# A decode step of attention beside a gated MLP: column groups of the output product, the last head's products and the final copy in two halves

## The chip, the cores and the metric

The kernel runs on one core of one Trainium2 chip. Its engines are TensorE (PE, with its weight loads as PEld), VectorE (DVE), ScalarE (ACT), GpSimd (POOL) and SyncE (SP); SyncE and ScalarE also issue DMA transfers, each on its own queue, and 16 DMA engines carry them. The metric is the device time in microseconds (us) of one execution. Before the change it was 662.07 us, the median of three runs (661.95 to 662.16).

## The reference

For a batch of 4 with one new token each (D = 640), the kernel adds three things:

```python
x = A_x                                    # 4 x 1 x 640, bf16
xn = _layernorm(x, axis=-1)
return x + _A_ref(xn, k_cache, v_cache, wq, wo) + _B_ref(xn, w_in, w_sp, b_sp, w_out)

# A: 32 heads of 128, caches of 4096 rows per batch and head
q = (x @ wq).reshape(B, 1, 32, 128)
p = softmax(q @ k.T * 128 ** -0.5)
return (p @ v).reshape(B, 1, 32 * 128) @ wo

# B: F = 1728, Fh = 864
z = gelu(x @ w_in)                         # tanh approximation
z1, z2 = z[..., :Fh], layernorm(z[..., Fh:])
return (z1 * (w_sp * z2 + b_sp)) @ w_out
```

The key and value caches are 4 x 32 x 4096 x 128 in bf16, 134 MB each. Everything else is small beside them.

## The kernel before

**Units.** The work is cut into 16 units: a group of 8 heads (`hg`, four of them) and one batch (`b`). A unit's keys are 8 x 4096 rows of 128, laid out over 128 partitions as 256 rows each (8 MB); its values likewise. Keys go to a ring of seven places in SBUF (`k_ring`, a quarter of a unit, 2 MB, in each place), values to `v_all`.

**Loads.** All loads of caches and weights go through SyncE's queue in a fixed list, `loads`. A function `pump()` issues as many of them as have their places free; every step of the main loop calls it. A place is taken when its load is issued and freed in the program once the last work that reads it has been put down; the instruction then waits by semaphore for that work. Ahead of the list stands the load of the query weights (L118). Behind the first two quarters of keys come the MLP's weights `w_in` (L127) and `w_out` (L124), which lie where values and products lie later. The first load of values (L175) can be issued only when the MLP is done with them. The last two units' loads are cut finer, so that the values of the last unit and the last group's output weights (L228, L231) come in pieces. The last head's weights come in two loads of 320 columns. The semaphores that count the landings of these loads are eight in number and are used in turn.

**Units in time.** In the main loop, VectorE multiplies a quarter of keys with the query, spread to all partitions (`product`, L537), and folds the product once (`fold_half`, L543); TensorE sums the rest with products against an identity (L555); VectorE reduces to scores (L569). Once a unit's scores are there, VectorE finds the maximum, ScalarE takes the exponentials (L596), VectorE spreads them by head (L607), and TensorE multiplies them with the values (L631). The order on TensorE, VectorE, ScalarE and SyncE is the one in which the program writes the instructions; GpSimd's is left to the scheduler.

**Start.** ScalarE's queue loads x (L101), TensorE puts x into the output sum (L373), VectorE computes the statistics (L265) and normalizes, TensorE transposes (L289) and multiplies with the query weights when they land (L303).

**The MLP.** `gmlp()` (L397) is a generator whose parts are put between the first steps of the main loop: products with `w_in` (L404), the tanh form of the GELU on VectorE and ScalarE (L414 to L432), the sums for its layer norm by a product with ones (L435), the statistics (L445 to L460), and the products with `w_out` (L503).

**The output sum.** One PSUM tile `out_ps` holds the output. Its 640 columns are held in two groups of 320: group 0 in partitions 0 to 3, group 1 in partitions 32 to 35 (`out_sum`, L369). x itself, the MLP and the four groups of heads (`group_proj`, L696) are summed into it by products of 320 columns for each group. The last group of heads ends the kernel: `o_n_last` (L817), 16 products (L699), one copy by ScalarE to SBUF (L823) and two transfers to the output, one from ScalarE's queue (L824) and one from SyncE's (L825).

Of the kernel before, what the change touches and what calls it, by code (L numbers as in the profile page):

```python
# [9 lines left out]
FP32 = mybir.dt.float32  # L10
BF16 = mybir.dt.bfloat16
ACT = mybir.ActivationFunctionType
ALU = mybir.AluOpType
# [4 lines left out]
def kernel(  # L18
# [14 lines left out]
    nc = tc.nc  # L33
    P = nc.NUM_PARTITIONS
    Bsz, Sq, D = A_x.shape
# [3 lines left out]
    Fh = F // 2  # L39
# [9 lines left out]
    HT = 8  # L49
    PAR = HT // NQ  # L50
    LN = P // HT
    HG = H // HT
# [17 lines left out]
    NOH = D // 2  # L70
# [10 lines left out]
    const = ctx.enter_context(tc.tile_pool(name="const", bufs=1))  # L81
# [18 lines left out]
    x_bf = ring[0:Bsz, 1, 0:D]  # L100
    nc.scalar.dma_start(out=x_bf, in_=A_x.flatten_outer_dims())  # L101
# [141 lines left out]
    for e in range(PAR):  # L243
        nc.gpsimd.tensor_copy(
            out=of_row[:, e, :, :, e, :],
# [8 lines left out]

    NACC = 2
# [113 lines left out]
    def out_sum(half):  # L369
        return out_ps[OG * half : OG * half + Bsz, :]  # L370

    for half in range(2):
        nc.tensor.matmul(  # L373
            out=out_ps[OG * half : OG * half + OG, :],
            lhsT=ident[:Bsz, :OG],
            rhs=x_bf[:, half * NOH : (half + 1) * NOH],
            start=True,
            stop=False,
        )
# [17 lines left out]
    def gmlp():  # L397
# [15 lines left out]
        for n, ks in by_lanes:  # L413
            nc.vector.tensor_copy(  # L414
                out=zz[0:n, :, k0 : k0 + ks, :], in_=zT[0:n, :, k0 : k0 + ks, :]
            )
# [6 lines left out]
        nc.scalar.activation(  # L423
            out=gt[:], in_=gw[:], func=ACT.Tanh, scale=math.sqrt(2.0 / math.pi)
        )
        yield
        nc.vector.tensor_scalar(
            out=gt[:], in0=gt[:], scalar1=1.0, scalar2=0.5, op0=ALU.add, op1=ALU.mult
        )
        nc.vector.tensor_tensor(out=gz[:, 0:2], in0=zz[:], in1=gt[:], op=ALU.mult)  # L430
# [5 lines left out]
            out=s_ps[:], lhsT=ones_sq[:, 0:1], rhs=gz[:, 1:3], start=True, stop=True  # L436
# [13 lines left out]
        )  # L450
        nc.vector.tensor_scalar(
            out=st[:, 0 : 2 * Bsz],
            in0=st[:, 0 : 2 * Bsz],
            scalar1=1.0 / float(Fh),
            scalar2=None,
            op0=ALU.mult,
# [239 lines left out]
    def group_proj(hg):  # L696
        for n, o in enumerate(gr.pop(hg)):
            for half in range(2):
                nc.tensor.matmul(  # L699
                    out=out_sum(half),  # L700
                    lhsT=o,
                    rhs=wo_sb[:, n, half * NOH : (half + 1) * NOH],
                    start=False,
                    stop=(hg == HG - 1 and n == HT - 1),
                )
        busy.remove(WO_AT)
# [26 lines left out]
    with tc.manual_schedule(engines={E.PE, E.DVE, E.Activation, E.SP}):  # L733
# [88 lines left out]
        out_v = out.flatten_outer_dims()  # L822
        nc.scalar.copy(out=res[0 : OG + Bsz], in_=out_ps[0 : OG + Bsz])  # L823
        nc.scalar.dma_start(out=out_v[:, 0:NOH], in_=res[0:Bsz])  # L824
        nc.sync.dma_start(out=out_v[:, NOH:D], in_=res[OG : OG + Bsz])  # L825
# [30 lines left out]
```

## Time and profile before

| | |
|---|---|
| median of three runs | 662.07 us |
| the profiled execution's own time | 662.09 us |
| its span (first to last instruction) | 660.2 us |
| DMA, mean over the span | 428 GB/s, 282.55 MB |
| VectorE busy | 522.6 us, 79% |
| TensorE busy | 317.0 us, 48% |
| ScalarE busy | 29.9 us, 5% |
| VectorE waiting for key loads at L537 | 87.9 us |

All times in views of the profile count from the span's start. The profile's page has six parts: busy time by engine, the span in 40 slices, the DMA queues, the chain of work that ended last, the costliest groups of instructions, and the DMA issues. A row of instructions gives start, length, engine, line, operation and tiles (out<-in), a count, and in brackets the idle time of the engine before it and what ended that. The chain follows each wait back to what released it. A row of a window gives the window, its length, each engine's busy time with its number of instructions, the clock granted to TensorE, the busy share of the DMA engines and their rate.

### The profile page before, as it was taken

Reading aid. Unit: us, or ns where it says so; the run is one execution under the profiler, and the core shown is the slowest. Engines: PE = TensorE matmul, PEld = TensorE weight load, DVE = VectorE, ACT = ScalarE, POOL = GpSimd, SP = SyncE. Lnnn points to the kernel's source line nnn. Section 1 sums busy time; section 2 is a strip of 40 time slices with the busy share of each in tenths; the row PEclk is TensorE's granted clock in tenths of the full one; section 3 lists DMA queues with packets and bytes.
Section 4 is the critical chain, followed back from the end, with each engine's and each line's share of the span. In section 5 each row is a group of like instructions: output and inputs, shape, how many; then the busy total and the mean of one; then the engine's idle time right before and its main releaser. Section 6 shows DMA issues by size and latency. Waiting matters only on the chain.

```text
span 660.2 us, 4777 instructions
## 1 busy us (share of the span) xinstructions
PE 317.0 (48%) x2083; PEld 136.3 (21%) x2083; DVE 522.6 (79%) x276; ACT 29.9 (5%) x73; POOL 10.1 (2%) x20
## 2 busy tenths in 40 slices
PE   0574372526427363452636336263452534737367
PEld 0231121212213121120212112121120211212124
DVE  1767978959597795969959598695969969999950
ACT  0020000000000000000000000000000000000000
POOL 2300000000000000000000000000000000000000
PEclk9757676766767676585767768676685867676785
DMA  9999999999999999999999999999999999999997
GB/s 369 433 461 434 417 441 434 433 437 438 421 445 426 437 430 441 437 422 433 434 441 441 418 437 441 430 441 421 434 441 437 426 421 445 422 427 436 449 409 284
DMA packets 8232, 282.55 MB, mean 428 GB/s; under 512 B 892, under 2 KB 2184, under 8 KB 2568
## 3 DMA queue, kind: packets, MB, share of 16 engines
q1 hardware_dynamic: 8192, 282.25, 99.1%
q8 instruction: 16, 0.26, 0.1%
q10 hardware_dynamic: 20, 0.01, 0.0%
q14 instruction: 4, 0.03, 0.0%
HBM read 282.24 MB, written 0.01 MB: 428 GB/s over the span
## 4 chain that ended last, share of the span: by engine, by line
DMA 62%; DVE 28%; PE 8%; issue 1%; ACT 0%; DVEq 0%
DMA k_ring<-in_A_k_cache_dram 53%; DVE k_ring L537 14%; DVE k_ring L543 7%; PE s_ps L555 6%; DMA v_all<-in_A_v_cache_dram 4%; DMA k_ring<-in_A_wo_dram 3%; DVE s_sb L569 3%; DMA v_all<-in_A_wq_dram 2%; DVE p_m L607 1%; DVE m L578 1%; PE q_ps L303 1%; PE pv L631 1%; PE out_ps L699 1%; DVE p_m L678 1%; DVE mf L580 1%
## 5 line engine op out<-in xcount | busy, mean ns | idle before, releaser
L537 DVE TENSOR_TENSOR k_ring<-k_ring,qbc 128x8192 bf16<-128x8192 bf16 x64 | 282.9, 4420 | 88.5 <-DMA k_ring<-in_A_k_cache_dram 87.9
L555 PE MATMUL s_ps<-k_ring,ident 128*128 128x512 bf16 x512 | 202.2, 566 | 313.8 <-DVE k_ring L543 313.7
L555 PEld LDWEIGHTS <-ident 128*128 128x128 bf16 x512 | 64.0, 130 | 430.0 <-issue 245.4
L543 DVE TENSOR_TENSOR k_ring<-k_ring 128x4096 bf16<-128x4096 bf16 x64 | 145.9, 2280 | 1.1
L631 PE MATMUL pv<-v_all,p_m 128*32 128x512 bf16 x960 | 62.5, 419 | 0.0
L569 DVE TENSOR_REDUCE s_sb<-s_ps 128x128 f32<-128x1024 f32 x32 | 39.0, 1218 | 3.7 <-PE s_ps L555 3.7
L607 DVE TENSOR_TENSOR p_m<-p_c,own 128x2048 bf16<-128x2048 bf16 x16 | 36.6, 2285 | 0.7 <-ACT p_c L596 0.7
L631 PEld LDWEIGHTS <-p_m 128*32 128x32 bf16 x992 | 26.6, 106 | 42.5 <-issue 23.3
L596 ACT ACTIVATE p_c<-s_sb,nm 128x256 bf16<-128x256 f32 x16 | 8.1, 508 | 342.9 <-DVE nm L588 342.9
L662 PEld LDWEIGHTS o_ps<-o_rows,pick 128*128 128x128 f32 x96 | 20.4, 294 | 4.3 <-issue 3.3
L662 PE MATMUL o_ps<-o_rows,pick 128*128 128x128 f32 x96 | 19.1, 367 | 0.0
L643 ACT COPY o_rows<-pv 128x512 f32<-128x512 f32 x16 | 9.4, 586 | 165.7 <-PE pv L631 165.7
L311 DVE TENSOR_SCALAR q_rows<-q_ps 128x512 bf16<-128x512 f32 x2 | 1.4, 692 | 12.8 <-PE q_ps L303 12.8
L817 DVE TENSOR_TENSOR o_n_last<-o_last,rden_all 128x32 bf16<-128x32 f32 x1 | 0.2, 192 | 12.2 <-PE o_last L809 12.2
L303 PE MATMUL q_ps<-v_all,xnT 128*32 128x512 bf16 x40 | 4.5, 630 | 9.3 <-DMA v_all<-in_A_wq_dram 9.3
L527 ACT CAST qbc<-qbc_ps 128x128 bf16<-128x128 f32 x16 | 4.3, 266 | 97.6 <-PE qbc_ps L519 97.6
L578 DVE TENSOR_REDUCE m<-s_sb 128x1 f32<-128x256 f32 x16 | 6.7, 420 | 0.5
L519 PE MATMUL qbc_ps<-q_rows,of_row 128*128 128x128 bf16 x32 | 6.0, 276 | 0.6 <-DVE q_rows L311 0.6
L519 PEld LDWEIGHTS <-of_row 128*128 128x128 bf16 x32 | 4.1, 132 | 8.1 <-issue 7.4
L716 PE MATMUL o_last<-hot,o_rows 128*128 128x8 f32 x32 | 4.9, 279 | 0.7 <-ACT o_rows L643 0.7
L716 PEld LDWEIGHTS o_last<-hot,o_rows 128*128 128x128 f32 x32 | 4.8, 226 | 1.8 <-ACT o_rows L643 1.6
L699 PE MATMUL out_ps<-k_ring,p_m 128*4 128x320 bf16 x48 | 4.0, 309 | 2.1 <-DVE p_m L691 2.1
(87 smaller groups left out, 81.4 us busy)
## 6 DMA issues: line engine op xcount, KB each, us to landing
k_ring<-in_A_k_cache_dram SPq DMA_DIRECT2D x5, 4096.0 KB, 27.2
v_all<-in_A_v_cache_dram SPq DMA_DIRECT2D x2, 4096.0 KB, 28.2
v_all<-in_A_wq_dram SPq DMA_DIRECT2D x1, 5120.0 KB, 15.4
k_ring<-in_A_k_cache_dram SPq DMA_DIRECT2D x2, 2048.0 KB
k_ring<-in_A_v_cache_dram SPq DMA_DIRECT2D x1, 4096.0 KB
k_ring<-in_A_wo_dram SPq DMA_DIRECT2D x3, 1280.0 KB, 20.6
v_all<-in_B_w_in_dram SPq DMA_DIRECT2D x1, 2160.0 KB
k_ring<-in_A_v_cache_dram SPq DMA_DIRECT2D x1, 2048.0 KB
```

The lines of the kernel that those rows point to most:

```text
L303: nc.tensor.matmul(out=q_ps[k * QD : (k + 1) * QD], lhsT=xnT[:, c, :], rhs=wq_v[:, c, k, e], start=(c == 0), stop=(c == DC - 1),)
L519: nc.tensor.matmul(out=qb_ps[:], lhsT=of_row[:, e, b].rearrange("p k f l -> p (k f l)"), rhs=q_rows[e][:, hg, :], start=(e == 0), stop=(e ...
L537: nc.vector.tensor_tensor(out=t, in0=t, in1=qbcs[u][:, None, :].to_broadcast([P, HC, Dh]), op=ALU.mult)
L543: nc.vector.tensor_tensor(out=t[:, :, 0:HD2], in0=t[:, :, 0:HD2], in1=t[:, :, HD2:Dh], op=ALU.add)
L555: nc.tensor.matmul(out=s, lhsT=ident[:], rhs=t[:, :, g * RW : (g + 1) * RW], start=(g == 0), stop=(g == m - 1),)
L569: nc.vector.tensor_reduce(out=scores[u][:].rearrange("p (r c) -> p r c", r=NK)[:, lo : hi + 1 : hi - lo], in_=sums_ps.pop(n // 2)[:], axis ...
L578: nc.vector.tensor_reduce(out=m1[:], in_=scores[u][:], axis=AX.X, op=ALU.max)
L607: nc.vector.tensor_tensor(out=p_m[:, u % 2], in0=p_c.pop(u)[:].rearrange("p (g c) -> p g c", c=CB)[:, :, :, None].to_broadcast([P, NG, CB, HT]
L631: nc.tensor.matmul(out=pvs[u][cg * QD : (cg + 1) * QD, :], lhsT=p_m[:, u % 2, g0 + n].rearrange("p c h -> p (c h)"), rhs=v_at[:, n * CB : ...
L662: nc.tensor.matmul(out=gr[hg][:], lhsT=pick[:, c, Bsz - 1 - b : P + Bsz - 1 - b], rhs=o[:, c, :], start=(b == 0 and c == 0), stop=(b == Bs ...
L699: nc.tensor.matmul(out=out_sum(half), lhsT=o, rhs=wo_sb[:, n, half * NOH : (half + 1) * NOH], start=False, stop=(hg == HG - 1 and n == HT ...
L716: nc.tensor.matmul(out=o_last[0][:, :, :, u % Bsz], lhsT=o[:, c, :], rhs=hot[:, c, :].rearrange("p (k e) -> p k e", e=PAR), start=(c == 0) ...
```

## The change

Five things are changed together.

- **Column groups.** The two groups of the output's columns are no longer the left and the right 320 columns. The 640 columns are cut into four blocks of 160; group 0 has blocks 0 and 2, group 1 has blocks 1 and 3. `columns(w, g)` picks them from the rows of a weight, and all products into `out_ps` use it.
- **The last head and the final copy.** The last head's two products of 320 columns become four of 160: both groups' first blocks, then both groups' second blocks. VectorE copies the first 160 columns of both groups, ScalarE the second. The two output transfers now write two pieces of 160 columns to each row.
- **x** is loaded with two transfers of two rows each, both on ScalarE's queue.
- **The GELU** is written with z halved on its way from PSUM and three operations of the form (a op scalar) op b, where there were five.
- **The mean** of the MLP's layer norm comes from a product with a column of 1/Fh in place of ones, and the scaling on VectorE goes. The column is one more small constant, set by GpSimd.

```diff
-    nc.scalar.dma_start(out=x_bf, in_=A_x.flatten_outer_dims())
+    x_rows = A_x.flatten_outer_dims()
+    for b0, b1 in ((0, 2), (2, 4)):
+        nc.scalar.dma_start(out=x_bf[b0:b1], in_=x_rows[b0:b1])
...
+    inv_fh = const.tile([P, 1], FP32)
+    nc.gpsimd.memset(inv_fh[:], 1.0 / float(Fh))
...
-    def out_sum(half):
-        return out_ps[OG * half : OG * half + Bsz, :]
+    NS = 2
+    NP = NOH // NS
+
+    def out_sum(g):
+        return out_ps[OG * g : OG * g + Bsz, :].rearrange("b (s n) -> b s n", s=NS)
+
+    def columns(w, g):
+        return w.rearrange("p (s g n) -> p g s n", s=NS, n=NP)[:, g]
...
-            rhs=x_bf[:, half * NOH : (half + 1) * NOH],
+            rhs=columns(x_bf, half),
...
-            nc.vector.tensor_copy(
-                out=zz[0:n, :, k0 : k0 + ks, :], in_=zT[0:n, :, k0 : k0 + ks, :]
+            nc.vector.tensor_scalar(
+                out=zz[0:n, :, k0 : k0 + ks, :],
+                in0=zT[0:n, :, k0 : k0 + ks, :],
+                scalar1=0.5, scalar2=None, op0=ALU.mult,
             )
-        nc.vector.tensor_tensor(out=gw[:], in0=zz[:], in1=zz[:], op=ALU.mult)
-        nc.vector.tensor_scalar(
-            out=gw[:], in0=gw[:], scalar1=0.044715, scalar2=1.0, op0=ALU.mult, op1=ALU.add
-        )
-        nc.vector.tensor_tensor(out=gw[:], in0=gw[:], in1=zz[:], op=ALU.mult)
+        nc.vector.scalar_tensor_tensor(
+            out=gw[:], in0=zz[:], scalar=4 * 0.044715, in1=zz[:], op0=ALU.mult, op1=ALU.mult
+        )
+        nc.vector.scalar_tensor_tensor(
+            out=gw[:], in0=gw[:], scalar=1.0, in1=zz[:], op0=ALU.add, op1=ALU.mult
+        )
...
-        nc.vector.tensor_scalar(
-            out=gt[:], in0=gt[:], scalar1=1.0, scalar2=0.5, op0=ALU.add, op1=ALU.mult
-        )
-        nc.vector.tensor_tensor(out=gz[:, 0:2], in0=zz[:], in1=gt[:], op=ALU.mult)
+        nc.vector.scalar_tensor_tensor(
+            out=gz[:, 0:2], in0=gt[:], scalar=1.0, in1=zz[:], op0=ALU.add, op1=ALU.mult
+        )
...
-            out=s_ps[:], lhsT=ones_sq[:, 0:1], rhs=gz[:, 1:3], start=True, stop=True
+            out=s_ps[:], lhsT=inv_fh[:], rhs=gz[:, 1:3], start=True, stop=True
...
-        nc.vector.tensor_scalar(
-            out=st[:, 0 : 2 * Bsz], in0=st[:, 0 : 2 * Bsz],
-            scalar1=1.0 / float(Fh), scalar2=None, op0=ALU.mult,
-        )
...
-                    rhs=w[:, half * NOH : (half + 1) * NOH],
+                    rhs=columns(w, half),
...
-            for half in range(2):
-                nc.tensor.matmul(
-                    out=out_sum(half),
-                    lhsT=o,
-                    rhs=wo_sb[:, n, half * NOH : (half + 1) * NOH],
-                    start=False,
-                    stop=(hg == HG - 1 and n == HT - 1),
-                )
+            last = hg == HG - 1 and n == HT - 1
+            for s in range(NS) if last else [None]:
+                for half in range(2):
+                    y, w = out_sum(half), columns(wo_sb[:, n, :], half)
+                    nc.tensor.matmul(
+                        out=y if s is None else y[:, s],
+                        lhsT=o,
+                        rhs=w if s is None else w[:, s],
+                        start=False,
+                        stop=last and s == NS - 1,
+                    )
...
-        out_v = out.flatten_outer_dims()
-        nc.scalar.copy(out=res[0 : OG + Bsz], in_=out_ps[0 : OG + Bsz])
-        nc.scalar.dma_start(out=out_v[:, 0:NOH], in_=res[0:Bsz])
-        nc.sync.dma_start(out=out_v[:, NOH:D], in_=res[OG : OG + Bsz])
+        rows = slice(0, OG + Bsz)
+        nc.vector.tensor_copy(out=res[rows, 0:NP], in_=out_ps[rows, 0:NP])
+        nc.scalar.copy(out=res[rows, NP:NOH], in_=out_ps[rows, NP:NOH])
+        out_v = out.flatten_outer_dims().rearrange("b (s g n) -> b g s n", s=NS, n=NP)
+        for g, dma in enumerate((nc.scalar, nc.sync)):
+            dma.dma_start(
+                out=out_v[:, g],
+                in_=res[OG * g : OG * g + Bsz].rearrange("b (s n) -> b s n", s=NS),
+            )
```

More of the change, by code (lines that the diff above doesn't have):

```diff
@@ L367 @@
     OG = 32
-    def out_sum(half):
-        return out_ps[OG * half : OG * half + Bsz, :]
+    NS = 2
[4 more added lines that the diff above has]
+        return w.rearrange("p (s g n) -> p g s n", s=NS, n=NP)[:, g]
     for half in range(2):
         nc.tensor.matmul(
-            out=out_ps[OG * half : OG * half + OG, :],
+            out=out_ps[OG * half : OG * half + OG, :].rearrange("b (s n) -> b s n", s=NS),
             lhsT=ident[:Bsz, :OG],
-            rhs=x_bf[:, half * NOH : (half + 1) * NOH],
+            rhs=columns(x_bf, half),
             start=True,
@@ L413, in gmlp @@
         for n, ks in by_lanes:
[L414 to L415 removed]
+            nc.vector.tensor_scalar(
+                out=zz[0:n, :, k0 : k0 + ks, :],
+                in0=zT[0:n, :, k0 : k0 + ks, :],
+                scalar1=0.5,
+                scalar2=None,
+                op0=ALU.mult,
             )
             k0 += ks
[L418 to L422 removed]
+        nc.vector.scalar_tensor_tensor(
+            out=gw[:], in0=zz[:], scalar=4 * 0.044715, in1=zz[:], op0=ALU.mult, op1=ALU.mult
+        )
+        nc.vector.scalar_tensor_tensor(
+            out=gw[:], in0=gw[:], scalar=1.0, in1=zz[:], op0=ALU.add, op1=ALU.mult
+        )
         nc.scalar.activation(
[L424 removed]
+            out=gt[:], in_=gw[:], func=ACT.Tanh, scale=2 * math.sqrt(2.0 / math.pi)
         )
         yield
[L427 to L428 removed]
+        nc.vector.scalar_tensor_tensor(
+            out=gz[:, 0:2], in0=gt[:], scalar=1.0, in1=zz[:], op0=ALU.add, op1=ALU.mult
         )
[L430 removed]
         sq = gz[:, 2, :, :]
@@ L449, in gmlp @@
             op=ALU.add,
-        )
-        nc.vector.tensor_scalar(
[L452 to L456, printed above, removed]
         )
```

## The prediction

> **What bounds the kernel now.** I read the page first, its slices and its DMA queues, then the chain of work that ended last, then the instructions in order of time at both ends of the span, then the groups by shape for prices.
>
> The slices and the queue rows of the page:
>
> ```profile
> DMA  9999999999999999999999999999999999999997
> GB/s 369 433 461 434 417 441 434 433 437 438 421 445 426 437 430 441 437 422 433 434 441 441 418 437 441 430 441 421 434 441 437 426 421 445 422 427 436 449 409 284
> ...
> q1 hardware_dynamic: 8192, 282.25, 99.1%
> ```
>
> The 16 DMA engines are busy in every slice but the last; SyncE's one queue fills 99.1% of them. A 64 KB piece takes 2.42 us, the same for over 99 in 100 of 3,456 of them. So the time is the bytes over a constant rate, plus what lies before the first packet and behind the last. VectorE is busy 79% but waits 87.9 us for caches at its large product, so no saving on it between the ends is worth anything.
>
> The end of the chain (start, length, what):
>
> ```profile
> 608.15 25.93 DMA v_all<-in_A_v_cache_dram
> 634.09 21.98 DMA k_ring<-in_A_wo_dram
> 656.07 0.04 issue
> 656.11 1.29 PE out_ps L699 x8
> ...
> 657.43 0.42 ACT v_all L823
> ```
>
> Behind the transfers stand the last eight products (four heads, two column groups), one copy on ScalarE, and the two output transfers up to 660.2. Only this tail, some 4 us, and the first microsecond are open to the change. The same tail in order of time:
>
> ```profile
> 654.48 2.91 PE L699 MATMUL out_ps<-k_ring,o_n_last 128*4 128x320 bf16 x16 [0.28 <-DVE o_n_last L817]
> ...
> 657.43 0.42 ACT L823 CAST v_all<-out_ps 36x320 bf16<-36x320 f32 x1 [9.36 <-PE out_ps L699]
> 657.87 0.30 SPq L825 DMA_DIRECT2D out_dram<-v_all  x1
> 657.88 0.28 ACTq L824 DMA_DIRECT2D out_dram<-v_all  x1
> ```
>
> TensorE releases ScalarE after 0.03 us; the issues follow 0.02 us after the copy. The prices come from the groups by shape (line, engine, operation, tiles, count, then busy us and mean ns), first VectorE's:
>
> ```profile
> L569 DVE TENSOR_REDUCE s_sb<-s_ps 128x128 f32<-128x1024 f32 x32 | 39.0, 1218 | 3.7 <-PE s_ps L555 3.7
> ...
> L311 DVE TENSOR_SCALAR q_rows<-q_ps 128x512 bf16<-128x512 f32 x2 | 1.4, 692 | 12.8 <-PE q_ps L303 12.8
> ...
> L414 DVE COPY zz<-zT 12x64 f32<-12x64 f32 x1 | 0.2, 202 | 0.0
> ```
>
> and ScalarE's:
>
> ```profile
> L643 ACT COPY o_rows<-pv 128x512 f32<-128x512 f32 x16 | 9.4, 586 | 165.7 <-PE pv L631 165.7
> ...
> L527 ACT CAST qbc<-qbc_ps 128x128 bf16<-128x128 f32 x16 | 4.3, 266 | 97.6 <-PE qbc_ps L519 97.6
> ...
> L823 ACT CAST v_all<-out_ps 36x320 bf16<-36x320 f32 x1 | 0.4, 420 | 9.4 <-PE out_ps L699 9.4
> ```
>
> The start, in order of time:
>
> ```profile
> 0.73 0.56 ACTq L101 DMA_DIRECT2D k_ring<-in_A_x_dram  x1
> ...
> 3.01 0.88 DVE L265 BATCH_NORM_STATS2 stats<-k_ring 4x6 f32<-4x320 bf16 x2 [3.01 <-DMA k_ring<-in_A_x_dram]
> ...
> 16.15 4.46 PE L303 MATMUL q_ps<-v_all,xnT 128*32 128x512 bf16 x40 [9.30 <-DMA v_all<-in_A_wq_dram]
> ...
> 46.29 0.33 SPq L175 DMA_DIRECT2D v_all<-in_A_v_cache_dram  x1
> ```
>
> **The change, part by part.**
>
> *The final copy.* One ScalarE copy of 320 columns becomes a VectorE copy of the first 160 and a ScalarE copy of the last 160. Read as written, the two could stand side by side. The built program of the changed kernel says otherwise. TensorE counts its semaphore up by 18 at the very last product (before: 14, 1 and 1 over the last three), and VectorE's copy waits for that full count, so it doesn't start on the first columns early. ScalarE's copy has no wait on TensorE at all: it waits for VectorE's count 274, which is VectorE's copy, its last instruction. So the copies stand one behind the other, and both output transfers wait for ScalarE's.
> Prices: VectorE from PSUM took 202 ns for 64 elements, 692 for 512, 1218 for 1024. The line from 64 to 512 gives 202 + 96 x 1.094 = 307 ns for 160, the line from 512 to 1024 run backwards 330; I take 0.32. ScalarE took 266 ns for 128 and 420 for 320: 0.80 ns an element, 0.29 us for 160. The hand-over from VectorE to ScalarE was 0.04 us at 69.6 and 0.09 at 638.1; I take 0.05. Sum 0.32 + 0.05 + 0.29 = 0.66 us where 0.42 stood: **+0.24**, bounds +0.20 to +0.29. Nothing hides it.
>
> *The last head's products.* Two of 320 columns become four of 160, each pair waiting for the landing of its half of that head's weights. Before, the last product alone waited for the last landing; now two of half the width do. The eight products start 0.13 us apart (656.11 to 657.0 for the eighth), and the groups, in different partitions, pass in pairs: 0.26 us a head. The same columns pass, so 0. Two more weight loads (PEld: 5 in 0.35 us, 0.07 each) give +0.14 if none is hidden; the gain is at most half a pair, -0.13. At L809 a product of 8 columns with its load came every 28 ns, so loads hide: I take 0.
>
> *The output transfers.* Each carries 8 pieces of 320 bytes for 4 of 640. The issue took 0.28 to 0.30 us for 4 pieces, and 0.39 at its shortest for a projection load of 256 pieces; a 640-byte packet took 29 to 34 ns. One more packet on an engine: +0.03, between -0.02 (shorter packets on more engines) and +0.1 (the longer issue). This lies on the path.
> The Trainium skill, "DMA: Bandwidth & Descriptors", Specifications, speaks against this part: below 512 bytes the engine does a read-modify-write. No run here shows one. With its 0.2 us for an access to HBM (section "Latency and other measured facts") the sum would be an estimated +0.47 in place of +0.27.
>
> *x in two loads.* ScalarE issues two instead of one, the second 0.3 to 0.56 us later. VectorE's statistics, which started at 3.01, start by about 3.6, and the transposed rows are ready by 7.8 instead of 7.2; TensorE waits for the query weights until 16.15, a cover of over 8 us. SyncE gains a wait: the load of w_out into v_all now waits for the first half of x, and the next w_out load for the second (before: for all of x). They were issued at 3.40 and 3.95, after x at 3.01. Behind them the key load waits for the query weights at 16.12 anyway. So 0 for both, until x lands past 16. The direct risk is at the engines: every nanosecond taken from one at the start is one more at its end. Of the four packets of x three took 53 to 60 ns and one 960, being among the first fetches; one more like it on the engine that ends last is +0.9, one fewer there is a gain, limited by the dribble at the end (below) to -0.5. I take 0, since the three are nearer.
>
> *Column groups, 160-column blocks.* The same products over the same elements, rows read as two runs of 160. The x and w_out products end some 600 us before the end; the projections of groups 0 to 2 (1.3 to 1.5 us each) lie under transfers that are 26 us in flight. 0; if they doubled, those transfers cover it.
>
> *The GELU part.* Eight VectorE instructions (two copies 0.41, 0.274, 0.219, 0.275, 0.219, 0.276, and 0.157 for the mean: 1.83 us) become five: two scaled copies at 0.22 by L419, three scalar-tensor-tensor at 0.274 (by L418) to 0.85 (by L678, the only rows of that operation). That is -0.6 to +1.2 us. Behind it waits the value load at 46.29; the key load issued at 32.04 lands at 63.03, which leaves 16.7 us. 0. One more GpSimd memset near 3 us (0.1) lies before that same wait: 0.
>
> *Where tiles lie.* The constant for the mean moves all later small tiles by 32 bytes, the query rows among them; the ring, the values and the products do not move. 0 (see the rivals).
>
> *Sum:* 0.24 + 0 + 0.03 = **+0.27 us**. The profiled execution took 662.09 (span 660.2 and 1.89 around it), 0.02 over the median of 662.07; I put the changed kernel at 662.09 + 0.27 = 662.36, against the median **662.3**. With all bounds of the tail (-0.13, +0.14, -0.02, +0.1, +0.20 to +0.29) the forecast's own range is 662.1 to 662.6. About 0.2%, 1.3 us, is what a measurement of this kernel can tell from no change; the tail's terms are all far below it.
>
> **The rivals.**
>
> 1. *The copies overlap, or the tail loses elsewhere what they cost.* Copies side by side would take 0.32, so -0.10 + 0.03: 662.0. For it: disjoint columns. Against: the wait named above. The Trainium skill, "PSUM — Partial Sum Buffer", section "PSUM bank collisions raise a hardware error", is on that side too: two engines on one bank and quadrant must be kept apart, reads against reads included; by that rule the serial sum stands, and no run here shows a collision.
> 2. *The output pieces are read before they are written.* Priced by the slowest cold packet here, 0.9 over its neighbours: 662.3 + 0.9 = 663.2. For it: the rule of the Trainium skill above. Against: 4-byte writes in the same queue take 9 to 25 ns.
> 3. *The start, either way.* A second cold packet on the last engine: 663.2; or one fewer, and less dribble. At the end the rate sinks in this way (window, its length, busy us, then clock, DMA share, GB/s):
>
> ```profile
> 654.40:654.60 0.20, 0.12 (x2) 0.09 (x4) 0.02 (x1) 0.00 (x0) 0.00 (x0) 0.50 1.06 354
> ...
> 655.60:655.80 0.20, 0.20 (x4) 0.04 (x1) 0.00 (x0) 0.00 (x0) 0.00 (x0) 0.50 0.53 163
> ...
> 656.40:656.60 0.20, 0.20 (x5) 0.14 (x2) 0.00 (x0) 0.00 (x0) 0.00 (x0) 0.50 0.07 22
> ```
>
> The engines end over 2 us; perfectly level they would end about 1 us earlier, but the eight products from 656.11 would follow only by what their own landings allow. 661.8.
> 4. *Slower by over 0.2%: the large product loses its rate.* Its second operand, the query rows, moves by 32 bytes. A unit costs VectorE 4 x 4.42 + 4 x 2.28 + 2 x 1.22 + 3.2 = 32.4 us against 38.8 of transfers, so it decides only when one product passes 6.0 us; at half its rate (8.84) 15 units of +11 us give about 830. For it: nothing shown. Against: the products of both buffers of the query rows agree within 0.1 us.
>
> **How the numbers follow.** Forecast 0.66; rival 1 0.10; rival 2 0.06, a third of it past 1.3 us; rival 3 0.12, evenly up and down, with 0.02 past the bound upward and 0.03 downward; rival 4 and what I have not seen 0.05, of which all is slower; 0.01 is left to slower as well. So slower 0.02 + 0.02 + 0.06 = 0.10, faster 0.03, the same 0.87. The range takes the forecast, rival 1 and the centres of rivals 2 and 3: 661.7 to 663.3, about 0.87 of the cases.
>
> **What would show it.** VectorE's copy starts 0.03 us after the last product and ScalarE's after VectorE's; 0.6 to 0.7 us from the end of the products to the issues. The last product ends within 0.15 us of 657.4 if the transfers end as before. The first large product starts near 21.95, the value load near 46. Wrong: copies that overlap, output packets over 0.1 us, last landings moved by over 0.5 us, or a mean of the large product other than 4.42.

## The result, and the profile after

The changed kernel takes a median of 662.81 us (662.48 to 663.16, 22 runs); the kernel before, run beside it, 661.99 us (661.74 to 662.19, 22 runs). The ratio is 1.0013, with a 95% interval of 1.0007 to 1.0018: 0.82 us slower, which is more than nothing and less than the 0.2% that the prediction took as its bound. The forecast was 662.3 with a range of 661.7 to 663.3, so the time lies in the range and the difference below the bound. The sum of the steps was +0.27, a third of what was measured.

The profiled execution of the changed kernel took 662.67 us with a span of 660.9; before it was 662.09 and 660.2. The rate of the transfers, from the slices and queue rows of the page after:

```profile
GB/s 368 436 457 433 424 432 438 424 444 437 432 428 445 424 429 436 440 433 413 441 440 437 429 421 444 429 440 440 433 416 444 437 436 424 416 442 417 452 415 266
...
q1 hardware_dynamic: 8196, 282.25, 99.0%
```

The same bytes pass at the same rate, so the body of the kernel has not moved. VectorE's large product, from the groups by shape after (line, engine, operation, tiles, count, then busy us and mean ns, then the idle time before it), has kept its 4.42 us although its query rows lie 32 bytes further on:

```profile
L545 DVE TENSOR_TENSOR k_ring<-k_ring,qbc 128x8192 bf16<-128x8192 bf16 x64 | 282.8, 4419 | 88.4 <-DMA k_ring<-in_A_k_cache_dram 87.8
```

The end of the chain of waits after (start, length, what):

```profile
634.05 21.89 DMA k_ring<-in_A_wo_dram
655.94 0.04 issue
655.98 1.25 PE out_ps L710 x10
657.23 0.02 issue
657.25 0.33 DVE v_all L834
657.58 0.02 issue
657.60 0.29 ACT v_all L835
```

The same tail after, in order of time, with the output transfers' issues (SPq and ACTq are the queues of SyncE and ScalarE):

```profile
654.35 2.86 PE L710 MATMUL out_ps<-k_ring,o_n_last 128*4 128x320 bf16 x18 [0.28 <-DVE o_n_last L828]
...
657.25 0.32 DVE L834 CAST v_all<-out_ps 36x160 bf16<-36x160 f32 x1 [2.96 <-PE out_ps L710]
657.60 0.29 ACT L835 CAST v_all<-out_ps 36x160 bf16<-36x160 f32 x1 [10.29 <-DVE v_all L834]
657.91 0.78 SPq L838 DMA_DIRECT2D out_dram<-v_all  x1
657.92 0.75 ACTq L838 DMA_DIRECT2D out_dram<-v_all  x1
```

The steps of the tail, read off these lines beside those of before (the spans, which the page rounds to 0.1 us, are 660.22 and 660.88 in the traces):

| step of the tail | before | after | difference |
|---|---|---|---|
| last product ends | 657.40 | 657.23 | -0.17 |
| from there to the issues (the copies) | 0.47 | 0.68 | +0.21 |
| issue of the output transfer, SyncE's | 0.30 | 0.78 | +0.48 |
| end of the issue to the end of the span | 2.05 | 2.19 | +0.14 |
| span | 660.22 | 660.88 | +0.66 |

The surprise is the issue. It took 0.78 us where the prediction had taken 0.30 with a little on top, and the end came 0.14 us later behind it as well: SyncE's first output packet started 0.90 us behind the end of its issue, before it was 0.52. The first row of the table is not shown to be an effect of the change; rival 3 below comes back to it.

The start, after (in order of time):

```profile
0.74 0.82 ACTq L103 DMA_DIRECT2D k_ring<-in_A_x_dram  x2
...
7.72 0.88 DVE L270 BATCH_NORM_STATS2 stats<-k_ring 4x6 f32<-4x320 bf16 x2 [7.72 <-DMA k_ring<-in_A_x_dram]
```

The second half of x landed at 7.72 us, not at the 3.6 that the prediction allowed.

### The profile page after: what moved, and what is told of

Read it like the earlier page. It is cut to its first block, busy times and chain, and to the rows that moved or that the text cites. A ratio compares the mean times of both kernels' runs of the same rounds, so it can differ in the third digit from the quotient of the medians.

```text
span 660.9 us, 4785 instructions
## 1 busy us (share of the span) xinstructions
PE 313.7 (47%) x2085; PEld 135.2 (20%) x2085; DVE 522.3 (79%) x274; ACT 29.7 (4%) x73; POOL 10.2 (2%) x21
## 4 chain that ended last, share of the span: by engine, by line
DMA 62%; DVE 28%; PE 8%; issue 1%; ACT 0%; DVEq 0%
DMA k_ring<-in_A_k_cache_dram 53%; DVE k_ring L545 14%; DVE k_ring L551 7%; PE s_ps L563 6%; DMA v_all<-in_A_v_cache_dram 4%; DMA k_ring<-in_A_wo_dram 3%; DVE s_sb L577 3%; DMA v_all<-in_A_wq_dram 2%; DVE p_m L615 1%; DVE m L586 1%; PE out_ps L710 1%; DVE p_m L686 1%; PE q_ps L308 1%; PE pv L639 1%; DVE mf L588 1%
## 5 line engine op out<-in xcount | busy, mean ns | idle before, releaser
L545 DVE TENSOR_TENSOR k_ring<-k_ring,qbc 128x8192 bf16<-128x8192 bf16 x64 | 282.8, 4419 | 88.4 <-DMA k_ring<-in_A_k_cache_dram 87.8
```

The source lines that it names most:

```text
L545: nc.vector.tensor_tensor(out=t, in0=t, in1=qbcs[u][:, None, :].to_broadcast([P, HC, Dh]), op=ALU.mult)
```

## Experiments

Three questions were open: which part of the change brings which share of the time, what about the output transfer costs its 0.62 us, and whether the copies could be made to pay. Times below are medians; each is set against the kernel before, run beside it (662.01 us for e1 to e4, 662.02 for e5 to e8, 661.97 for e9 to e11).

### The parts alone

**e1_front.** The kernel before with the start and the GELU of the change, and nothing of the column groups or the tail.

```diff
-    nc.scalar.dma_start(out=x_bf, in_=A_x.flatten_outer_dims())
+    x_rows = A_x.flatten_outer_dims()
+    for b0, b1 in ((0, 2), (2, 4)):
+        nc.scalar.dma_start(out=x_bf[b0:b1], in_=x_rows[b0:b1])
...
+    inv_fh = const.tile([P, 1], FP32)
+    nc.gpsimd.memset(inv_fh[:], 1.0 / float(Fh))
...
+        nc.vector.scalar_tensor_tensor(
+            out=gw[:], in0=zz[:], scalar=4 * 0.044715, in1=zz[:], op0=ALU.mult, op1=ALU.mult
+        )
```

> The front alone: x in two loads, the GELU in three operations, the mean from a column of 1/Fh, and the small constant that moves the later tiles by 32 bytes. The end is that of the kernel before: column halves, one copy on ScalarE, output pieces of 640 bytes. If the loss of 0.82 us lies in the tail, as I read the two traces, this runs at the time before within 0.1 us (ratio 1.0000). If the second half of x, which landed at 7.7 us in the changed kernel, or the order of the first packets costs, it is slower by 0.3 us or more.

Measured: 661.88 us (661.76 to 662.15), ratio 0.9998 (0.9989 to 1.0007). The start and the GELU cost nothing; the 0.13 us below the kernel before lie inside the interval.

**e2_copies.** The kernel before with the last head's products and the final copy in two halves, VectorE and ScalarE, and with the groups and the output transfers left as they were (4 pieces of 640 bytes).

```diff
+            for c0, c1 in ((0, NP), (NP, NOH)) if last else ((0, NOH),):
+                for half in range(2):
+                    nc.tensor.matmul(
+                        out=out_sum(half)[:, c0:c1],
...
-        nc.scalar.copy(out=res[0 : OG + Bsz], in_=out_ps[0 : OG + Bsz])
+        rows = slice(0, OG + Bsz)
+        nc.vector.tensor_copy(out=res[rows, 0:NP], in_=out_ps[rows, 0:NP])
+        nc.scalar.copy(out=res[rows, NP:NOH], in_=out_ps[rows, NP:NOH])
```

> The kernel before with the last head's products in four pieces of 160 columns and the final copy in two column halves, VectorE then ScalarE; the groups stay left and right halves, so the output pieces are 640 bytes as before. If the serial copies cost what the prediction said, the copies take 0.32 + 0.03 + 0.29 and the time is the one before +0.2 to +0.3 us (ratio 1.0003 to 1.0004), with output issues at 0.28 to 0.30 us. If the copies have a larger effect, for example on how long the issue behind them takes, it reaches +0.8 us.

Measured: 662.43 us (662.24 to 662.71), ratio 1.0006 (0.9997 to 1.0015). Its tail in order of time:

```profile
657.25 0.32 DVE L827 CAST v_all<-out_ps 36x160 bf16<-36x160 f32 x1 [3.10 <-PE out_ps L702]
657.60 0.28 ACT L828 CAST v_all<-out_ps 36x160 bf16<-36x160 f32 x1 [9.79 <-DVE v_all L827]
657.91 0.30 SPq L830 DMA_DIRECT2D out_dram<-v_all  x1
657.91 0.27 ACTq L829 DMA_DIRECT2D out_dram<-v_all  x1
```

The copies stand one behind the other as in the changed kernel, and the issues have their old 0.30 us. From the last product to the issue it is 0.2 us more than before. By the medians it is 0.42, with an interval from -0.2 to +1.0 us, so the trace is the sharper of the two.

**e3_pieces.** The kernel before with the alternate-block groups and the output transfers that follow from them, with the last head's products and the single copy left alone.

```diff
+    def columns(w, g):
+        return w.rearrange("p (s g n) -> p g s n", s=NS, n=NP)[:, g]
...
-        nc.scalar.dma_start(out=out_v[:, 0:NOH], in_=res[0:Bsz])
-        nc.sync.dma_start(out=out_v[:, NOH:D], in_=res[OG : OG + Bsz])
+        out_v = out.flatten_outer_dims().rearrange("b (s g n) -> b g s n", s=NS, n=NP)
+        for g, dma in enumerate((nc.scalar, nc.sync)):
+            dma.dma_start(
+                out=out_v[:, g],
+                in_=res[OG * g : OG * g + Bsz].rearrange("b (s n) -> b s n", s=NS),
+            )
```

> The kernel before with the column groups of alternate 160-column blocks and the output transfers of eight 320-byte pieces each; products of 320 columns and one copy on ScalarE as before. If the output issue is the missing term, both issues take 0.75 to 0.78 us here too and the time is the one before +0.5 to +0.65 us (ratio 1.0008 to 1.0010). If it is not, the issues take 0.3 us and the time is that of before within 0.1 us.

Measured: 662.66 us (662.53 to 662.91), ratio 1.0010 (1.0001 to 1.0019): +0.65 us. Its output transfers, from the answer for their line (minimum, median and maximum in ns, then first and last start):

```profile
L831 SPq DMA_DIRECT2D out_dram<-v_all x1: 777/777/777, 657.9 to 657.9; - x1
L831 ACTq DMA_DIRECT2D out_dram<-v_all x1: 754/754/754, 657.9 to 657.9; - x1
```

This part alone brings most of the loss. The three parts add up to -0.13 + 0.42 + 0.65 = +0.94 us, against +0.82 for all of them together.

### What in the output transfer costs

**e4_four_small.** e3 with only the first block of each group written, so that each transfer has 4 pieces of 320 bytes in a pattern of two steps (rows, columns) in place of 8 in three (rows, blocks, columns).

```diff
-                out=out_v[:, g],
-                in_=res[OG * g : OG * g + Bsz].rearrange("b (s n) -> b s n", s=NS),
+                out=out_v[:, g, 0],
+                in_=res[OG * g : OG * g + Bsz, 0:NP],
```

> As the run of the pieces alone, but each output transfer carries only the first block of its group: four pieces of 320 bytes, a pattern of two steps that the built program marks as prepared ahead, as it does for the kernel before and not for the changed one. The second blocks of the output are not written. If the issue is dear because of the form of the transfer, it takes 0.28 to 0.30 us here and the time is that of before within 0.1 us. If pieces under 512 bytes are dear as such, the issue, or the way from the issue to the landing, stays 0.3 us or more above the kernel before (+0.3 to +0.6 us). If the number of pieces decides, the issue is at 0.3 us too; the next run tells that from the form.

Measured: 661.85 us (661.76 to 662.15), ratio 0.9997 (0.9989 to 1.0006). The same view of it:

```profile
L831 SPq DMA_DIRECT2D out_dram<-v_all x1: 299/299/299, 657.8 to 657.8; - x1
L831 ACTq DMA_DIRECT2D out_dram<-v_all x1: 278/278/278, 657.8 to 657.8; - x1
```

With pieces of the same 320 bytes the issue is back at 0.30 us and the whole loss is gone; its runs and e3's do not overlap. So the size of a piece, and with it a read before each write, is not the cause. In the changed kernel itself the packets of 320 bytes took 18 to 20 ns, less than those of 640 bytes before (29 to 34).

**e6_sixteen_pieces.** e3 with blocks of 80 columns, so 16 pieces of 160 bytes to a transfer.

```diff
-    NS = 2
+    NS = 4
```

> As the run of the pieces alone, but with blocks of 80 columns: each output transfer has sixteen pieces of 160 bytes in one pattern of three steps. If the issue is dear by its form, it takes 0.75 to 0.8 us as with eight pieces, and the time is that of before +0.5 to +0.7 us. If it grows with the number of pieces (0.28 for four, 0.76 for eight, so 0.12 a piece), it takes about 1.7 us and the time is that of before +1.5 us.

Measured: 662.77 us (662.45 to 662.99), ratio 1.0011 (1.0002 to 1.0020). The same view of it:

```profile
L831 SPq DMA_DIRECT2D out_dram<-v_all x1: 781/781/781, 657.8 to 657.8; - x1
L831 ACTq DMA_DIRECT2D out_dram<-v_all x1: 753/753/753, 657.8 to 657.8; - x1
```

Twice the pieces take the same issue as 8, so the count is not the cause either. What is left is the form of the transfer, or how the built program prepares a transfer of that form.

**e5_four_transfers.** e3 with each output transfer as two of the two-step form, one behind the other on its queue.

```diff
-            dma.dma_start(
-                out=out_v[:, g],
-                in_=res[OG * g : OG * g + Bsz].rearrange("b (s n) -> b s n", s=NS),
-            )
+            for c in range(NS):
+                dma.dma_start(
+                    out=out_v[:, g, c],
+                    in_=res[OG * g : OG * g + Bsz, c * NP : (c + 1) * NP],
+                )
```

> As the run of the pieces alone, but with four output transfers in place of two, two behind each other on each queue, each of four pieces of 320 bytes in the two-step form. All of the output is written. If the form decides, each issue takes 0.25 to 0.3 us, the second of a queue ends about 0.55 us after the copy in place of 0.76, and the time is that of before +0.25 to +0.35 us, less than with the two transfers of eight. If small pieces are dear, the two issues together take 0.75 us or more and nothing is gained.

Measured: 662.32 us (662.19 to 662.75), ratio 1.0005 (0.9996 to 1.0014). Two issues on a queue, from its instructions in order of time:

```profile
657.75 0.65 SPq L832 DMA_DIRECT2D out_dram<-v_all  x2
657.75 0.63 ACTq L832 DMA_DIRECT2D out_dram<-v_all  x2
```

Two issues of some 0.30 us with a gap take less than one of 0.78, and about half of the 0.65 us comes back. The other half is the second issue, which nothing hides here.

The built programs show more. Each transfer there either carries a mark that it was prepared ahead or does not. The output transfers of two steps carry it, those of three steps don't. In the kernel before, the only transfers without it are four loads of w_out of three rows each, and the answer for their line had their price (minimum, median, maximum in ns):

```profile
L124 SPq DMA_DIRECT2D p_m<-in_B_w_out_dram x5: 463/651/819, 3.9 to 28.2; - x5
```

The shortest of the five is the one load with the mark; the four others took 0.65 to 0.82 us. Marked loads of keys ahead of and behind them, at 16.12 and 32.04 us, took 0.33 and 0.34. This is the row from which the output transfers should have been priced.

These loads also tell the mark from the steps, since they are without the mark and have two steps only (rows, columns). The other way round, three of the four loads of the last group's output weights have three steps (partitions, heads, columns) and carry the mark:

```profile
L228 SPq DMA_DIRECT2D k_ring<-in_A_wo_dram x4: 388/3232/8577, 621.6 to 643.8; - x4
```

The shortest, 0.39 us, is the first of the three, and it took 0.39 us in all 13 traces. What the longer ones behind it wait for is not shown; the one with two steps is among them, at 4.53 us. So the long issue goes with the missing mark and not with the number of steps. No run changed the mark alone, so that the mark is the cause stays argued.

### Could the copies pay?

**e7_quarters.** The kernel before with four groups of 160 columns, each in a quarter of the partitions of `out_ps`. ScalarE copies the two lower quarters, VectorE the two upper; the output transfers keep their 4 pieces of 640 bytes.

```diff
-    out_ps = ps_out.tile([P, NOH], FP32)
+    out_ps = ps_out.tile([P, NP], FP32)
...
+    def block(q):
+        b = NS * (q % 2) + q // 2
+        return slice(b * NP, (b + 1) * NP)
...
+            for q in (0, 2, 1, 3) if last else range(NB):
...
-        nc.scalar.copy(out=res[0 : OG + Bsz], in_=out_ps[0 : OG + Bsz])
+        rows = OG + Bsz
+        nc.scalar.copy(out=res[0:rows, 0:NP], in_=out_ps[0:rows])
+        nc.vector.tensor_copy(out=res[0:rows, NP:NOH], in_=out_ps[2 * OG : 2 * OG + rows])
```

> Another way to the same halves: the output sum in four groups of 160 columns, in the four quarters of the partitions, so that four products pass TensorE side by side; ScalarE copies the lower two, VectorE the upper two beside them, so that a row of the output lies together in SBUF and the output pieces are 640 bytes again. In the built program VectorE's copy waits for ScalarE's, both reading one PSUM tile. The last eight heads' products should shrink: the last four heads took 1.29 us with pairs at 0.26, and with fours at 0.13 they would take 0.8, if the landings allow it. So -0.3 to -0.5 for the products, +0.24 for the copies, and the time is that of before -0.25 to 0 us. If the four products don't pass side by side, it is +0.24 us or more.

Measured: 663.61 us (662.22 to 663.87), ratio 1.0021 (1.0012 to 1.0030). Its tail in order of time:

```profile
655.89 0.43 PE L708 MATMUL out_ps<-k_ring,o_n_last 128*4 128x160 bf16 x8 [0.39 <-DMA k_ring<-in_A_wo_dram]
657.83 0.71 PE L708 MATMUL out_ps<-k_ring,o_n_last 128*4 128x160 bf16 x8 [1.51 <-DMA k_ring<-in_A_wo_dram]
658.58 0.28 ACT L833 CAST v_all<-out_ps 36x160 bf16<-36x160 f32 x1 [10.73 <-PE out_ps L708]
658.90 0.33 DVE L834 CAST v_all<-out_ps 36x160 bf16<-36x160 f32 x1 [4.72 <-ACT v_all L833]
```

Two things happen. The copies are serial again: the built program makes VectorE wait for ScalarE although their partitions differ. And the last products wait 1.51 us, until 657.83, for a load whose last packet ended at 657.71, over a microsecond later than before (656.63). The four products of a head did pass side by side: where no load held them, eight products, those of two heads, took 0.43 us. The second had nothing to do with the question and got experiments of its own, below.

**e8_two_banks.** e7 with the two upper quarters in a second tile of PSUM.

```diff
-    ps_m = ctx.enter_context(tc.tile_pool(name="ps_m", bufs=2, space=PSUM))
+    ps_m = ctx.enter_context(tc.tile_pool(name="ps_m", bufs=1, space=PSUM))
...
-    out_ps = ps_out.tile([P, NP], FP32)
+    out_ps = [ps_out.tile([P, NP], FP32, name=f"out{n}") for n in range(2)]
```

> As the run before, but the two upper quarters lie in a second PSUM tile, in another bank (which one of the two small PSUM buffers gives up), so that VectorE's and ScalarE's copies wait for TensorE alone. If the order of the copies is what cost 0.24 us, both start within 0.2 us of the end of the products and the issue follows 0.35 us after it: about 0.3 us faster than the run before and -0.3 to -0.6 us against the kernel before (ratio 0.9991 to 0.9996). If the small buffer that was given up is needed, waits appear in the main loop and the time rises by more than 0.5 us.

Measured: 663.31 us (661.99 to 663.53), ratio 1.0019 (1.0009 to 1.0028). Its profiled execution, at 662.21 us one of two among eleven that were that quick, shows the tail without the late load:

```profile
656.18 1.20 PE L708 MATMUL out<-k_ring,o_n_last 128*4 128x160 bf16 x16 [0.38 <-DMA k_ring<-in_A_wo_dram]
657.41 0.29 ACT L833 CAST v_all<-out 36x160 bf16<-36x160 f32 x1 [9.42 <-PE out L708]
657.45 0.33 DVE L834 CAST v_all<-out 36x160 bf16<-36x160 f32 x1 [2.88 <-PE out L708]
```

Here the copies run side by side. From the last product (657.38) to the issue (657.84) it is 0.46 us, where one ScalarE copy before had 0.47. So splitting the copy over two engines has next to nothing to win, even where it works. The last four heads' products took 1.20 us, before it was 1.29, and not the 0.8 that was expected for e7. The small buffer was not missed: VectorE waited 88.3 us for key loads, 87.9 before.

### The late load of e7 and e8

TensorE's instructions come in pieces of 16 KB through the same 16 DMA engines that carry the data. The page counts them in a queue of their own, and e7 and e8 have 17 of them where before had 16: their built programs have 4,174 instructions on TensorE in place of 3,986. One fetch took 0.88 to 0.97 us of an engine, and a 64 KB data piece beside one took 2.89 to 2.97 us in place of 2.42. Either the 17th puts one engine behind the others, or the times at which the fetches fall do.

**e9_fetch_same.** The kernel before with 256 more instructions on TensorE, where TensorE has time to spare: the broadcast of the query row is made five times over for each unit.

```diff
     def stage_q(u):
...
-        for e in range(PAR):
+        for e in list(range(PAR)) * (5):
```

> The kernel before with the small products that spread a unit's query (two a unit) written five times over instead of once, for all 16 units: 128 more products with their weight loads, 256 more TensorE instructions, hidden in the main loop beside transfers; the output is the same. In the traces so far TensorE's instructions come in fetches of 16 KB through the same 16 DMA engines, 16 such fetches of about 0.93 us in the kernel before (the last at 654.56) and 17 in the two kernels with four groups (the last at 655.66 and 656.27, with the last weights of the output landing up to 1.5 us later). Theory one, that the number counts: 17 fetches, and one engine ends about 0.5 us later, +0.2 to +0.6 us. Theory two, that only a fetch among the last loads counts: the last fetch should keep its place near 654.5, and the time is that of before within 0.15 us. Theory three, that the fetches have nothing to do with it: no change, wherever the last one lies.

Measured: 663.04 us (662.80 to 663.32), ratio 1.0016 (1.0008 to 1.0025): +1.07 us. The queue row of its page, then its tail in order of time:

```profile
q8 instruction: 17, 0.28, 0.1%
```

```profile
654.38 1.41 PE L699 MATMUL out_ps<-k_ring,o_n_last 128*4 128x320 bf16 x8 [0.28 <-DVE o_n_last L817]
657.13 1.24 PE L699 MATMUL out_ps<-k_ring,o_n_last 128*4 128x320 bf16 x8 [1.33 <-DMA k_ring<-in_A_wo_dram]
658.42 0.42 ACT L823 CAST v_all<-out_ps 36x320 bf16<-36x320 f32 x1 [10.42 <-PE out_ps L699]
```

Its last windows (window, its length, busy us of TensorE, its weight loads, VectorE, ScalarE and GpSimd, the clock, the DMA share, GB/s):

```profile
656.60:656.80 0.20, 0.00 (x0) 0.00 (x0) 0.00 (x0) 0.00 (x0) 0.00 (x0) 0.50 0.07 26
657.00:657.20 0.20, 0.07 (x2) 0.07 (x3) 0.00 (x0) 0.00 (x0) 0.00 (x0) 0.50 0.06 19
```

The first of them in the kernel before:

```profile
656.60:656.80 0.20, 0.20 (x4) 0.18 (x2) 0.00 (x0) 0.00 (x0) 0.00 (x0) 0.50 0.00 0
```

There the DMA share is 0.00. Here it stays at 0.06 to 0.07, which is one engine of sixteen, up to the last packet at 657.52. The last fetch kept its place (654.66 us, before it was 654.56), so theory two, which then allowed 0.15 us, is false. The last head's weights are complete only then, and the tail hangs on this one engine.

**e10_fetch_late.** The same, but not for the first unit, so that the fetches fall at other times.

```diff
-        for e in list(range(PAR)) * (5):
+        for e in list(range(PAR)) * (5 if u else 1):
```

> As the run before, but for 15 of the 16 units: 240 more TensorE instructions, so that the 17th fetch comes 16 instructions later in the tail, among the last eight heads' products, near 655.5 to 656.3. Theory two (place): the last weights land 0.5 to 1.5 us later than 656.6 in most executions, and the time is that of before +0.5 to +1.5 us, with the spread that the kernel with four groups showed (662.2 to 663.9). Theory one (number): the same as the run before, +0.2 to +0.6 us. Theory three: no change.

Measured: 663.06 us (662.93 to 663.29), ratio 1.0017 (1.0008 to 1.0026), again 17 fetches (the last at 654.96 us, in e9 at 654.66), and the last load's packet at 657.49. The last fetch came far earlier than was expected of this run (655.5 to 656.3), so it adds little on the place of the fetches. Their number is what goes with the loss in these two runs, in the direction that was expected and at twice the size. The number alone does not decide it, since the quick execution of e8 has 17 fetches too and no late load. That the late engine is the one with the 17th fetch is argued: the trace does not name the engine of a packet.

### The change, repaired

**e11_repaired.** The changed kernel with e5's four output transfers, nothing else.

```diff
         for g, dma in enumerate((nc.scalar, nc.sync)):
-            dma.dma_start(
-                out=out_v[:, g],
-                in_=res[OG * g : OG * g + Bsz].rearrange("b (s n) -> b s n", s=NS),
-            )
+            for s in range(NS):
+                dma.dma_start(
+                    out=out_v[:, g, s],
+                    in_=res[OG * g : OG * g + Bsz, s * NP : (s + 1) * NP],
+                )
```

> The changed kernel with one thing mended: four output transfers of four 320-byte pieces, two behind each other on each queue, in place of two of eight pieces. If the form of the output transfer is the term that the prediction missed, this takes off what the pair of runs on the pieces showed (662.66 against 662.32, 0.34 us): 662.4 to 662.55, between the kernel before and the changed one's 662.81. If the loss has another source, it stays at 662.8.

Measured: 662.05 us (661.97 to 662.50), ratio 1.0003 (0.9994 to 1.0012): 0.08 us above the kernel before, where the changed kernel is 0.82 above it. Its tail in order of time:

```profile
657.26 0.32 DVE L834 CAST v_all<-out_ps 36x160 bf16<-36x160 f32 x1 [2.96 <-PE out_ps L710]
657.61 0.68 SPq L839 DMA_DIRECT2D out_dram<-v_all  x2
657.61 0.28 ACT L835 CAST v_all<-out_ps 36x160 bf16<-36x160 f32 x1 [9.77 <-DVE v_all L834]
657.62 0.64 ACTq L839 DMA_DIRECT2D out_dram<-v_all  x2
```

This gave back more than was expected of it, and the lines show why. The first transfer of each queue needs only VectorE's half, so both are issued at 657.61 and 657.62, beside ScalarE's copy. The last issue ends at 658.29, 0.40 us earlier than in the changed kernel and 0.12 later than before, and from there to the end of the span it is 1.95 us in place of 2.19. The serial copies then cost little, because the first half's transfer fills the time of the second copy. No version here beats the kernel before by more than its runs spread.

## Why the prediction was right, and where its sizes were wrong

*What bounds the kernel.* Right. The transfers kept their rate, and the difference in the spans lies in the tail; the time moved by 0.82 us in 662.

*The final copy: +0.24 (0.20 to 0.29).* Right. VectorE took 0.32 us, ScalarE 0.29, with 0.03 between them; from the last product to the issues the tail grew by 0.21. The order of the two was read from the waits of the built program, and the trace has it so. On rival 1, copies that overlap: false for this kernel, and the two-tile run showed that its -0.10 was too kind as well, since the gain side by side was 0.01.

*The last head's products: 0.* Right. From the last load's packet to the last product it was 0.77 us before (656.63 to 657.40) and 0.73 after (656.50 to 657.23).

*The output transfers: +0.03 (-0.02 to +0.1).* This is the step that failed, and the term that was mis-sized. It measured +0.48 us in the issue and +0.14 behind it in the trace, and +0.65 us by the run that had this part alone. The prediction bounded the issue by the number of its pieces, "0.39 at its shortest for a projection load of 256 pieces". That load carries the mark of a transfer prepared ahead, and the new output transfers do not. Their price was in the trace of before, in the loads of w_out without the mark at 0.65 to 0.82 us, and the built program of the changed kernel showed which of the two kinds the new transfers would be. With 0.45 for the issue the sum would have been about 0.7.

*Rival 2: the pieces are read before they are written, 663.2.* False as a mechanism, although it ended nearer to the result than the forecast's own term for this part. The Trainium skill, "DMA: Bandwidth & Descriptors", Specifications, has a read-modify-write below 512 bytes. The run with 4 pieces of 320 bytes took 661.85 us against 662.01, and the packets of 320 bytes 18 to 20 ns, so no run here shows such a cost. A nearer total for the wrong reason would have sent the repair to the size of the pieces; the repair that works keeps them at 320 bytes.

*x in two loads: 0.* The cost is right, the account was not. The statistics waited until 7.72 us, not 3.6; the second transfer's packets landed among those of the first weights. The next w_out load did not wait for x at all, but for the query weights, at 16.61. The cover was large enough: the query weights' products started at 16.64 (16.15 before), and the first value load was issued at 45.48, before it at 46.29. The start alone took 661.88 us against 662.01.

*Rival 3: the start, either way.* The last load's packet came 0.13 us earlier (656.50 against 656.63), far from the 0.9 of a cold packet on the last engine and from the -0.5 of a level end. Nothing says that the changed start brings these 0.13 us. The run with the start alone had its last packet at 656.48, but e2 to e6, which keep the old start, had theirs at 656.39 to 656.62. So the 0.13 us, and with them the -0.17 in the first row of the table, lie in what one execution differs from another.

*Column groups: 0.* Right. In the run with the groups and the output transfers, the last group's products took 2.93 us, before it was 2.91.

*The GELU: -0.6 to +1.2 of cover.* Its three new operations took 0.28 us each, at the low end of the bounds, and the row of 0.85 us that set the upper one did not apply. Nothing of it reaches the end.

*Rival 4: the large product loses its rate.* False: 4,419 ns against 4,420.

So the sum that the trace shows is -0.17 for the last product, +0.21 for the copies, +0.48 for the issue and +0.14 behind it: +0.66, which is the difference of the spans. Without the first, which is not shown to be of the change, it is +0.83, and the medians differ by 0.82. The copies came out within their bounds; the last two are the failed term. The difference stayed below 0.2% because the tail's terms are small beside 1.3 us, also when one of them was off by a factor of twenty. That the range holds the time is in part luck: the forecast's own range of 662.1 to 662.6 does not, and the stated one reached to 663.3 for rivals 2 and 3, neither of which took place.

## What to carry to other kernels

Price a changed transfer at the end of a kernel not only by its bytes and pieces: see in the built program whether it is prepared ahead like those it replaces, and look in the trace for issues of the same kind, the longest rows as well as the shortest. Two transfers that are prepared ahead can be cheaper than one that is not, above all where the first can leave beside the work that the second waits for. Where the time is the data transfers' rate, count also what else passes through their engines, and instructions most of all: TensorE work that is hidden in time can still cost a fetch.

## What the runs showed of the hardware that was not expected

- The issue of an output transfer took 0.27 to 0.31 us in the two-step form, which the built program marks as prepared ahead, and 0.75 to 0.78 in the three-step form without the mark, with 8 or with 16 pieces. Loads of two steps without the mark took 0.65 to 0.82 us, and a load of three steps with it 0.39.
- 240 to 256 more instructions on TensorE, in time that TensorE had to spare, cost 1.07 to 1.09 us: with the 17th fetch of 16 KB one DMA engine of sixteen goes on to 657.52 or 657.49, where the last packet before came at 656.63. What stays open is whether the fetches go round the engines in turn, so that the 17th falls on one that has had its share, and why two of eleven executions each of the two quarter kernels, with 17 fetches as well, took only 662.0 to 662.3 us.
- ScalarE and VectorE don't read one tile of PSUM side by side in the built program, even in different partitions (0.32 us between their starts); from two tiles they start 0.04 us apart.
- The second half of a small load, issued 0.6 us behind the first half, landed at 7.72 us where the whole load had landed at 3.01, among the first packets of the weights; in the two other runs with the load in halves it was 7.94 and 7.91.
